# Reads of the memory in the ring of the projections: one PSUM tag changed in an attention and token-mixing kernel

## The chip, the core and the metric

The kernel runs on one core of one Trainium2 chip. The metric is the device time of one execution in microseconds (us). TensorE (PE) multiplies and writes its results into PSUM; VectorE (DVE) and ScalarE (ACT) read them from there; GpSimd (POOL) works on the on-chip memory SBUF; SyncE (SP) issues the DMAs. Each engine runs its own list of instructions in order and waits on semaphores for the others.

## What is computed

A layer norm with modulation, an attention with a compressive memory over four segments, a residual, a second layer norm, and a token-mixing MLP (7 products of a two-level block scheme stand in for its matrix products). Only the attention matters here:

```python
for s in range(N):                       # 4 segments of 512 tokens, 32 heads of 32
    p = softmax(qs @ ks.T * scale + mask)
    a_dot = p @ vs
    pq = phi(qs)                          # phi(t) = t + 1 if t > 0 else exp(t)
    num = pq @ M                          # what the queries read from the memory
    den = pq @ z + 1e-6
    o = g * num / den + (1 - g) * a_dot
    pk = phi(ks)
    M = M + pk.T @ vs                     # the memory's update
    z = z + pk.sum(over tokens)
```

## The kernel before

**Work.** The attention runs over 32 iterations `t`, each of them one group of four heads (`g`) and one segment (`seg`). Iterations 0 to 15 take segments 0 and 1 of the eight groups in turn, iterations 16 to 31 segments 2 and 3. Each iteration has

- a projection (`project`): 96 matmuls for keys and values in two halves (`nps`, L192, 48 each), four transposes of the keys (`kps`, L405) and 24 matmuls for the queries (`qps`, L200). ACT and DVE split each result into a high and a low part (L119, L122). Where the segment is not 0, ACT makes a relu (L416) and an exponential (L417) of the queries and DVE makes `pq` of them (L419);
- the memory (`memory`): for a segment other than 0 two reads `rd` (L450; two halves of two matmuls each) that need `pq` and the memory `MZ`. DVE adds a constant to their denominators (L452), inverts (L453) and multiplies into `am` (L454). Up to segment 2 an update `up` follows (L460, four matmuls), which DVE masks (L462 or L465);
- for each of four heads the maxima (L478 on PE, L480 on DVE; every second head a small transpose `nmps`, L486, and two DMAs of the maxima back into `sk`), the scores (`a`, L515 to L522 on PE; exponentials on ACT; masking, a cast and a subtraction on POOL and ACT, L526 to L530) and the values (`pv`, L544, twenty matmuls; L547 to L551 on DVE), and once an output transpose `ops` (L559).

24 of the 32 iterations have a segment other than 0 and so read the memory: the odd ones up to 15, and all from 16 on.

**PSUM.** There are eight banks, and `bank(tag, bufs, name)` hands them out in rings: `pj` has two, `s1` two (maxima), `s2` two (scores), `pv` one, `ms` one. A tile of a ring of n buffers takes the place of the one that was handed out n calls earlier with the same tag, and its first writer waits until the last reader of that one is done. Before, `pj` carries `nps` half 0, `nps` half 1, `kps`, `qps`, and then `nps` of the next iteration. `ms` carries the two `rd`, `up`, two `nmps` and `ops`.

**Order.** The main loop runs over 128 heads `n`. It calls scores for head `n`, maxima for head `n + 3`, values for head `n - 2` and a piece of the projection for head `n + 8`, so that an iteration is projected two iterations ahead of its scores:

```python
    for n in range(-LEADS, 4 * NI + VL):
        at(scores, n)
        at(maxima, n + LEADS)
        at(values, n - VL)
        m = n + LEADP
        ...
        if m >= 8:
            at(project, m)
```

This gives priorities, not the final order. When the kernel is built, a scheduler goes through a simulated time and gives each engine the first piece that is ready, by the dependencies of tiles and of ring buffers. A dependency that is changed can thus reorder every engine's list.

Of the kernel before, what the change touches and what calls it, by code (L numbers as in the profile page):

```python
# [41 lines left out]
def attention_and_mlp(ctx, tc, x, wq, wkv, wo, beta, w1, b1, w2, b2, c, wm_a, wm_b, out):  # L42
# [19 lines left out]
    a = par.__enter__()  # L62
# [9 lines left out]
    def bank(tag, bufs, name):  # L72
        return psum.tile([P, 512], F32, tag=tag, bufs=bufs, name=name)
# [246 lines left out]
    for i in range(2):  # L320
        ps = bank("s2", 2, f"scps{i}")
# [20 lines left out]
    pj = prj.__enter__()  # L342
# [35 lines left out]
    def project(t, piece):  # L378
# [50 lines left out]
        else:  # L429
# [7 lines left out]
            A.copy(vp[:, :, :, 33:65], r1)  # L437
            V.tensor_tensor(vp[:, :, :, 65:97], r1, vp[:, :, :, 33:65], op=ALU.subtract)
            memory(t)

    def memory(t):
        pr, g, seg = its[t]
        d = st[t]
        d["am"] = am = b.tile([P, 4, 128], F32, tag="am", bufs=3, name=f"am{t}")
        if seg:
            for half in range(2):
                ps = bank("ms", 1, f"rd{t}_{half}")[:, 0:264].rearrange("p (a n) -> p a n", a=2)
                for aa in range(2):
                    i = 2 * half + aa
                    T.matmul(ps[:, aa], d["pq"][:, 128 * i:128 * i + 128], MZ[:, g], start=True, stop=True)  # L450
                rd = b.tile([P, 2, 4], F32, tag="rd", bufs=2, name=f"rdd{t}_{half}")
                V.tensor_scalar_add(rd, ps[:, :, 128:132], 1e-6)  # L452
                V.reciprocal(rd, rd)  # L453
                V.tensor_tensor(am[:, 2 * half:2 * half + 2].rearrange("p a (h e) -> p a h e", h=4),  # L454
                                ps[:, :, 0:128].rearrange("p a (h e) -> p a h e", h=4),
                                rd.unsqueeze(3).to_broadcast([P, 2, 4, 32]), op=ALU.mult)
        if seg < 3:
            ps = bank("ms", 1, f"up{t}")
            for i in range(4):
                T.matmul(ps[:, 0:132], d["pk"][:, i], d["v32"][:, i], start=(i == 0), stop=(i == 3))  # L460
            if seg == 0:
                V.tensor_tensor(MZ[:, g], ps[:, 0:132], bdg[:, g], op=ALU.mult)  # L462
            else:
                tm = b.tile([P, 132], F32, tag="tm", bufs=1, name=f"tm{t}")
                V.tensor_tensor(tm, ps[:, 0:132], bdg[:, g], op=ALU.mult)  # L465
                G.tensor_tensor(MZ[:, g], MZ[:, g], tm, op=ALU.add)
# [132 lines left out]
    def seg_load(seg):  # L599
        seg_x[seg] = [load_x(s2p, tt) for tt in range(4 * seg, 4 * seg + 4)]  # L600
        return norm_all(seg_x[seg])
# [9 lines left out]
    with tc.issue_after(last_wm.ins):  # L611
        _, exp, _, normed_v = seg_load(1)
# [58 lines left out]
    for g in range(2, NG):  # L671
        n = 8 * g - 13
# [5 lines left out]
    for j in range(32):  # L678
        n = ML0 + 2 * j + (8 if j >= 8 else 0)
        later(n, lambda j=j: mod_fetch(j), n + (2 if j < 8 else 1), lambda r, j=j: mod_late(j, r), "V")  # L680
    plan(WO0 - 3, lambda: spread(gaw, 0))
    for i in range(8):
        n = WO0 + WOS * i
        later(n, lambda i=i: wo_fetch(i), n + 1, lambda r, i=i: wo_split(i, r), "G")

    for n in range(-LEADS, 4 * NI + VL):
# [4 lines left out]
        if 0 <= m + 4 < 4 * NI:  # L691
            t = (m + 4) // 4
# [79 lines left out]
    def product(tt):  # L772

        r = wr_.tile([P, NK, P], F32, tag="otr", bufs=1, name=f"otr{tt}")
        SY.dma_start(r, oT[:, :, P * tt:P * tt + P].rearrange("g p n -> p g n"))
        os_ = ws_.tile([P, 2, D], F32R, tag="ots", bufs=2, name=f"ots{tt}")
        for j in range(2):
            split(os_[:, :, 512 * j:512 * j + 512], r[:, 4 * j:4 * j + 4].rearrange("p a b -> p (a b)"), A, V)
        x1 = w.tile([P, D], F32, tag="x1", bufs=2, name=f"x1_{tt}")
        load = SY.dma_start(x1, x[P * tt:P * tt + P])  # L780
        if tt == 1:
            with tc.issue_after(load.ins):
                for c in range(5, NK):
                    SY.dma_start(wop[c, 1].bitcast(F32), wos[c, 1])

        def half(nh):
            ps = bank("pj", 2, f"po{tt}_{nh}")
            n = 0
            for ct in range(NK):
                for i, j in ((0, 0), (0, 1), (1, 0)):  # L790
                    T.matmul(ps, os_[:, i, P * ct:P * ct + P], wop[ct, nh][:, j], start=(n == 0), stop=(n == 3 * NK - 1))  # L791
                    n += 1
            c0, c1 = 512 * nh, 512 * nh + 512
            V.scalar_tensor_tensor(x1[:, c0:c1], ps, 1.0, x1[:, c0:c1], op0=ALU.mult, op1=ALU.add,
                                   accum_out=x1s[:, 2 * tt + nh:2 * tt + nh + 1])
            if nh:
                kept[tt] = SY.dma_start(x1d[tt], x1)

        return half
# [49 lines left out]
    for products, tt in (((0, 1), 0), ((2,), 1), ((3, 4, 8), 8), ((9,), 9), ((10,), 2), ((11,), 10), ((12,), 3),  # L849
# [5 lines left out]
        for i in products:  # L855
            if i > 1:
                f = product(i)
# [283 lines left out]
```

## Time and profile before

| | us |
|---|---|
| runs: median of three (lowest, highest) | 2231.71 (2225.53, 2231.82) |
| the profiled execution's own time | 2226.6 |
| its span | 2224.9 |
| PE busy in the span | 2190.3 (98%) |
| DVE busy | 1666.7 (75%) |
| ACT busy | 1135.7 (51%) |
| POOL busy | 725.8 (33%) |

The attention fills the span up to about 956 us, the output projection follows up to about 1153 us, and the MLP takes the rest. Spans are those of one execution, taken by the hardware profiler. Matmuls are pipelined and their ends are modelled, so that two matmuls in a row overlap in the records. What one costs on PE is the distance to the start of the next.

### The profile page before, as it was taken

How to read it: one execution, taken by the hardware profiler on the slowest of the kernel's cores; microseconds unless marked ns; L12 is line 12 of the kernel's file. 1: busy time of each engine (PE TensorE's matmuls, PEld its weight loads, DVE VectorE, ACT ScalarE, POOL GpSimd, SP SyncE). 2: the span in 40 equal slices, each digit the busy share in tenths (PEclk: the TensorE clock that was granted, in tenths of full speed). 3: DMA queues.
4: the chain of work that ended last, by engine and by line, in shares of the span. 5: the costliest groups of instructions: out<-in, count | busy, mean ns of one | idle time of the engine just before them, and what ended most of it. 6: DMA issues, size and time to landing. Idle time of an engine off the chain costs nothing.

```text
span 2224.9 us, 38052 instructions
## 1 busy us (share of the span) xinstructions
PE 2190.3 (98%) x13786; PEld 1881.0 (85%) x13786; DVE 1666.7 (75%) x3762; ACT 1135.7 (51%) x2050; POOL 725.8 (33%) x831
## 2 busy tenths in 40 slices
PE   8999999999999999999999999999999999999999
PEld 5988898888999999888888888888888888888887
DVE  7676777756777777664858766888888886969687
ACT  5486776756666666654636533533334242424232
POOL 2175766646767776663002200033330000000000
PEclk9999999999999999999999999999999999999999
DMA  7666666686556666664754687655556542414134
GB/s 287 192 187 191 175 181 193 189 279 216 170 180 205 188 183 211 193 219 143 231 194 186 226 304 275 243 223 220 204 202 219 206 148 64 145 57 147 57 123 151
DMA packets 175183, 423.03 MB, mean 190 GB/s; under 512 B 17524, under 2 KB 71828, under 8 KB 166036
## 3 DMA queue, kind: packets, MB, share of 16 engines
q1 hardware_dynamic: 174996, 420.61, 57.5%
q8 instruction: 109, 1.79, 0.3%
q14 instruction: 78, 0.64, 0.1%
HBM read 244.62 MB, written 125.06 MB: 166 GB/s over the span
## 4 chain that ended last, share of the span: by engine, by line
PE 87%; DVE 5%; DMA 3%; ACT 2%; POOL 1%; issue 1%; SPq 0%; DVEq 0%; ACTq 0%
PE mx L921 48%; PE nps L192 11%; PE po L791 8%; PE qps L200 7%; PE pv L544 3%; PE a L515 1%; PE sz L478 1%; PE sx L478 1%; DMA sk<-nt 1%; PE up L460 1%; PE a L518 1%; POOL p L530 1%; PE a L522 1%; PE sy L478 1%; PE rd L450 1%
## 5 line engine op out<-in xcount | busy, mean ns | idle before, releaser
L921 PE MATMUL mx<-bU,sp 128*128 128x512 f32 x2352 | 534.3, 389 | 0.9 <-DVE ac L928 0.9
L921 PEld LDWEIGHTS mx<-bU,sp 128*128 128x128 f32 x2352 | 441.3, 188 | 93.4 <-issue 1.3
L119 ACT CAST sp<-wr 128x384 fp32r<-128x384 f32 (+2 forms) x408 | 218.1, 547 | 431.8 <-PE mx L921 349.1
L192 PE MATMUL nps<-wv,h 128*128 128x256 f32 x3072 | 431.2, 283 | 1.6 <-DVE h L122 0.7
L921 PE MATMUL mx<-bA,sp 128*128 128x512 f32 x1764 | 430.5, 389 | 0.0
L530 POOL TENSOR_TENSOR p<-p,ph 128x640 f16<-128x640 f32 x256 | 380.2, 1485 | 138.5 <-ACT ph L528 134.5
L192 PEld LDWEIGHTS nps<-wv,h 128*128 128x128 f32 x3072 | 400.3, 189 | 9.4 <-DVE h L122 2.0
L921 PEld LDWEIGHTS mx<-bA,sp 128*128 128x128 f32 x1764 | 331.2, 188 | 68.7
L122 DVE TENSOR_TENSOR sp<-wr,sp 128x384 fp32r<-128x384 f32 (+2 forms) x408 | 259.8, 648 | 24.7 <-ACT sp L119 24.4
L928 DVE TENSOR_TENSOR ac<-mx,ac 128x512 f32<-128x512 f32 x280 | 189.9, 687 | 85.2 <-PE mx L921 84.1
L200 PE MATMUL qps<-h,wq 128*128 128x512 f32 x768 | 197.9, 400 | 0.0
L528 ACT CAST ph<-p 128x1280 f16<-128x1280 f32 x128 | 161.4, 1261 | 59.7 <-POOL p L526 59.6
L791 PE MATMUL po<-wo,ots 128*128 128x512 f32 x768 | 180.9, 391 | 0.0
L791 PEld LDWEIGHTS po<-wo,ots 128*128 128x128 f32 x768 | 142.7, 188 | 28.7
L200 PEld LDWEIGHTS qps<-h,wq 128*128 128x128 f32 x768 | 141.6, 190 | 27.7
L921 PE MATMUL mx<-bB,sp 128*128 128x512 f32 x588 | 164.0, 389 | 0.0
L526 POOL TENSOR_SCALAR_AFFINE_SELECT p<-p 128x256 f32<-128x256 f32 x256 | 134.1, 529 | 81.8 <-ACT p L523 53.9
L921 PEld LDWEIGHTS mx<-bB,sp 128*128 128x128 f32 x588 | 110.4, 188 | 22.9
L480 DVE CUSTOM_DVE_ANT_0 sz<-sz,mask 128x512 f32<-128x512 f32 x128 | 89.1, 696 | 52.0 <-PE sz L478 49.5
L480 DVE CUSTOM_DVE_ANT_0 sx<-sx,mask 128x128 f32<-128x128 f32 (+1 forms) x256 | 93.7, 366 | 44.1 <-PE sx L478 37.9
L928 DVE TENSOR_TENSOR cc<-mx,cc 128x512 f32<-128x512 f32 x140 | 94.9, 684 | 37.6 <-PE mx L921 37.4
L516 ACT ACTIVATE p<-a,shift 128x512 f32<-128x512 f32 x128 | 88.4, 691 | 41.2 <-PE a L515 40.4
(209 smaller groups left out, 3244.7 us busy)
## 6 DMA issues: line engine op xcount, KB each, us to landing
sk<-sg SPq DMA_DIRECT2D x384, 128.0 KB
wr<-in_w_dram SPq DMA_DIRECT2D x28, 1024.0 KB
wr<-in_w_dram SPq DMA_DIRECT2D x32, 768.0 KB
bstu<-ucd SPq DMA_DIRECT2D x28, 768.0 KB
wsp<-wv SPq DMA_DIRECT2D x32, 512.0 KB
rawm<-in_wm_b_dram SPq DMA_DIRECT2D x32, 512.0 KB
wv<-wsp SPq DMA_DIRECT2D x32, 512.0 KB
pcd<-cc SPq DMA_DIRECT2D x14, 1024.0 KB
```

Of the source, the lines that this page charges most:

```text
L119: last_hi[0] = A.copy(hi, src)
L122: return lo_eng.tensor_tensor(lo, src, hi.bitcast(F32), op=ALU.subtract)
L192: T.matmul(ps[:, aa], h[:, j, 128 * tt:128 * tt + 128], wt[:, i, o:o + 256], start=(n == 0), stop=(n >= 6 * NK - 2), skip_group_check=True)
L200: T.matmul(ps, wt[:, i, o:o + 128], h[:, j], start=(k + n == 0), stop=(3 * k + n == 3 * NK - 1))
L480: marks[4 * t + h - LEADS, "V"] = V.tensor_tensor_reduce(o, o, mask[:, 384 - 128 * i:], 1.0, -3.0e38, op0=ALU.add, op1=ALU.max, accum_out= ...
L516: A.activation(p32[:, 0:512], b0, AF.Exp, scale=SCALE, bias=shift)
L526: G.affine_select(w, w, pattern=[[0, 2], [1, 128]], compare_op=ALU.is_ge, fill=0.0, base=0, channel_multiplier=-1)
L528: marks[n, "A"] = A.copy(hi, p32)
L530: marks[n, "G"] = G.tensor_tensor(lo[:, c], p32[:, c], hi[:, c], op=ALU.subtract)
L791: T.matmul(ps, os_[:, i, P * ct:P * ct + P], wop[ct, nh][:, j], start=(n == 0), stop=(n == 3 * NK - 1))
L921: T.matmul(ps, ops[q][:, i, P * k:P * k + P], b[:, j], start=(m == 0 and first), stop=(m == 3 * nk - 1), skip_group_check=True)
L928: V.tensor_tensor(d, ps, d, op=ALU.add)
```

## The change

The two reads of an iteration take their PSUM bank from the ring `pj` of two buffers in place of the ring `ms` of one:

```diff
         if seg:
             for half in range(2):
-                ps = bank("ms", 1, f"rd{t}_{half}")[:, 0:264].rearrange("p (a n) -> p a n", a=2)
+                ps = bank("pj", 2, f"rd{t}_{half}")[:, 0:264].rearrange("p (a n) -> p a n", a=2)
                 for aa in range(2):
                     i = 2 * half + aa
                     T.matmul(ps[:, aa], d["pq"][:, 128 * i:128 * i + 128], MZ[:, g], start=True, stop=True)
```

In an iteration that reads, `pj` now hands out six tiles: `nps` 0, `nps` 1, `kps`, `qps`, `rd` 0, `rd` 1. `nps` half 0 of the next iteration takes the bank of `rd` 0, and half 1 that of `rd` 1. `ms` is left with `up`, `nmps` and `ops`. The instructions are the same; the scheduler puts them in another order on every engine, from iteration 1 to the last heads of the attention.

The first place is PE's list in iteration 25 (group 4, segment 3), a few instructions behind its last query matmul. `nps_0_11965` and `nps_1_12090` are the key and value projection of iteration 26, `rd_0_11881` and `rd_1_11888` the two reads of iteration 25, `a_...` scores and `s..._` maxima. Before:

```order
L192 MATMUL nps_0_11965<-wv_5_1_1_11523,h_6_7307 128x256 x4
L450 MATMUL rd_0_11881<-MZ,pq_11802 128x132 x2
L521 MATMUL a_23_2_11708<-sk_2_503 128x128
L522 MATMUL a_23_2_11708<-sk_2_503 128x256
L478 MATMUL sy_3_11920<-sk_3_500 128x384
L515 MATMUL a_23_3_11817<-sk_3_504 128x512
L192 MATMUL nps_0_11965<-wv_5_1_1_11523,h_6_7307 128x256 x2
L192 MATMUL nps_0_11965<-wv_5_1_1_11523,h_7_7762 128x256 x6
L192 MATMUL nps_1_12090<-wv_5_0_0_11517,h_0_6929 128x256 x6
```

and in the changed kernel, at the same reads:

```order
L478 MATMUL sy_3_11920<-sk_3_500 128x384
L515 MATMUL a_24_0_11900<-sk_0_497 128x512
L518 MATMUL a_24_0_11903<-sk_0_497 128x384
L521 MATMUL a_24_0_11906<-sk_0_497 128x128
L522 MATMUL a_24_0_11906<-sk_0_497 128x256
L450 MATMUL rd_0_11881<-MZ,pq_11802 128x132 x2
L450 MATMUL rd_1_11888<-MZ,pq_11802 128x132 x2
L515 MATMUL a_24_1_12029<-sk_1_498 128x512
L478 MATMUL sz_3_11923<-sk_3_500 128x512
L518 MATMUL a_24_1_12032<-sk_1_498 128x384
L478 MATMUL sx_0_12045<-sk_0_501 128x128
L478 MATMUL sx_0_12045<-sk_0_501 128x256
```

Before, 40 of the 48 matmuls of `nps_0_11965` stand ahead of the first read. In the changed kernel all 96 stand behind both reads, and between the last query matmul and the first of them stand only pieces of heads (here three `L515`, three `L518`, two pairs of `L521` and `L522`, three pairs of `sx`, two `sy`, two `sz`, one `nmps` and forty `pv` matmuls) and the reads.

The second place is DVE's list in the same iteration. Before, from the subtraction that makes the low part of the queries (`sg_11764<-qps_11772`) on:

```order
L122 TENSOR_TENSOR sg_11764<-qps_11772,sg_11764 128x512
L436 TENSOR_TENSOR r_25_11874<-v_25_11530,vp_11873 128x512
L489 SCALAR_TENSOR_TENSOR nt_24_1_11731<-nmps_1_11728,nt_24_1_11730 8x128
L419 SCALAR_TENSOR_TENSOR pq_11802<-qps_11772,rq_11799 128x512
L480 ISA sz_2_11841,mx_2_11832<-sz_2_11841,mask 128x512
L480 ISA mx_2_11832 128x1
L573 SCALAR_TENSOR_TENSOR rawm_11813,mcol<-rawm_11813,scb 128x1024
```

In the changed kernel thirteen rows stand between that subtraction and `pq`: two pieces of `sx`, a `sy` and a `sz` with a short row of the accumulator behind each, and `L436`, `L547`, `L489`, `L573` and `L549`. From `pq` to the eviction of the first read it then reads:

```order
L419 SCALAR_TENSOR_TENSOR pq_11802<-qps_11772,rq_11799 128x512
L438 TENSOR_TENSOR vp_11873<-r_25_11874,vp_11873 128x16x32
L480 ISA sy_3_11920,mx_2_11832<-sy_3_11920,mask 128x384
L480 ISA mx_2_11832 128x1
L480 ISA sx_3_11915,mx_2_11832<-sx_3_11915,mask 128x256
L480 ISA mx_2_11832 128x1
L551 SCALAR_TENSOR_TENSOR red_1_11866<-red_1_11866,gate,pv_1_11844 128x128
L452 TENSOR_SCALAR rdd_0_11884<-rd_0_11881 128x8
L453 RECIPROCAL rdd_0_11884<-rdd_0_11884 128x8
L454 TENSOR_TENSOR am_11880<-rd_0_11881,rdd_0_11884 128x256
```

Before, `pq` was third behind the subtraction; now it is fourteenth, because the maxima that PE runs in that stretch have moved ahead of it.

## The prediction

> **What bounds the kernel now.** I first read the busy time by stage (columns: stretch in us, its length, then busy time with the number of instructions for PE, weight loads, DVE, ACT and POOL; then the granted TensorE clock, the DMA share and GB/s), here the two halves of the attention:
>
> ```profile
> 60.00:525.00 465.00, 451.35 (x3898) 412.84 (x3899) 332.56 (x968) 318.06 (x587) 274.71 (x315) 0.99 0.66 197
> 525.00:956.00 431.00, 424.87 (x3845) 391.25 (x3844) 307.87 (x938) 275.05 (x476) 294.52 (x354) 1.00 0.64 194
> ```
>
> PE is busy 451.35 of 465.00 us and 424.87 of 431.00 us, so it waits 13.65 + 6.13 = 19.8 us in the whole attention; DVE and ACT have about a quarter of the time free. The attention lasts as long as PE's list. Whatever leaves PE without work lengthens the kernel, and a shorter wait elsewhere gives back 19.8 us at the very most. Next I read PE's timeline at the place that the change touches, iteration 25, behind its last query matmuls (start, length, engine, line, matmul; the distance from a start to the next is the cost):
>
> ```profile
> 782.27 0.71 PE L200 MATMUL qps<-h,wq 128*128 128x512 f32 x2
> 782.82 0.39 PE L478 MATMUL sx<-sk 96*128 96x128 f32 x2
> 783.05 0.34 PE L478 MATMUL sy<-sk 96*128 96x384 f32 x1
> 783.23 1.78 PE L192 MATMUL nps<-wv,h 128*128 128x256 f32 x14
> ...
> 786.19 0.48 PE L515 MATMUL a<-sk 98*128 98x512 f32 x1
> 786.51 0.34 PE L518 MATMUL a<-sk 98*128 98x384 f32 x1
> 786.68 0.39 PE L478 MATMUL sz<-sk 96*128 96x512 f32 x1
> 786.91 0.44 PE L544 MATMUL pv<-vp,ph 128*128 128x97 bf16 x6
> ...
> 787.50 0.48 PE L478 MATMUL sx<-sk 96*128 96x128 f32 x2
> ...
> 789.76 0.61 PE L450 MATMUL rd<-MZ,pq 128*128 128x132 f32 x4
> 790.12 0.31 PE L521 MATMUL a<-sk 98*128 98x128 f32 x1
> ...
> 790.44 0.34 PE L478 MATMUL sy<-sk 96*128 96x384 f32 x1
> ```
>
> The queries end at 782.27 + 0.71 = 782.98, and at 783.23, after one `sx` and one `sy`, the projection of iteration 26 begins. The reads wait for `pq`, which ACT and DVE make out of those queries; PE runs the projection in the meantime, and the first read comes at 789.76. That is the cover that matters: the 6.8 us from the queries' end to the read are filled with PE work, mostly `nps`.
>
> **The change part by part.** Nothing is removed or added: the same matmuls, evictions and DMAs are issued. What changes is two dependencies, and by them the order.
>
> *First: reads and updates no longer share one bank.* `up` waits no longer for the second read's eviction, nor do `nmps` and `ops` queue behind reads in `ms`. The largest such wait in the trace is this (in brackets the idle time before, and who ended it):
>
> ```profile
> 455.29 2.10 PE L460 MATMUL up<-v,pk 128*128 128x132 f32 x8 [3.48 <-DVE am L454]
> ```
>
> 3.48 us once. I count this gain inside the 19.8 us below and not by itself.
>
> *Second: the next projection waits for the reads.* `nps` half 0 takes the bank of `rd` 0, so its first matmul cannot start before DVE's L454 has read that bank. Behind it on PE stand 96 matmuls and everything after them. In the 24 iterations that read, the order therefore puts only pieces of heads between the last `qps` and the first `nps`, and the question is whether they fill the chain queries, `pq`, read, eviction. The last of the 24 has no `nps` behind it, which leaves 23.
>
> The chain, for iteration 25 in the changed order, by the mean duration of each kind of instruction between 600 and 905 us (number, busy time, then mean ns of one; idle time behind the bar):
>
> ```profile
> L480 DVE CUSTOM_DVE_ANT_0 sz<-sz,mask 128x512 f32<-128x512 f32 x44 | 30.7, 697 | 13.9 <-PE sz L478 13.8
> L573 DVE SCALAR_TENSOR_TENSOR rawm<-rawm,scb 128x1024 f32<-128x1024 f32 x20 | 30.0, 1501 | 6.7 <-DMA rawm<-in_wm_b_dram 6.7
> L480 DVE CUSTOM_DVE_ANT_0 sy<-sy,mask 128x384 f32<-128x384 f32 x44 | 25.3, 575 | 0.9 <-PE sy L478 0.7
> L480 DVE DVE_READ_ACCUMULATOR2_ANT mx<- 128x1 f32 x173 | 24.3, 140 | 0.0
> L549 DVE TENSOR_REDUCE red<-pv 128x128 f32<-128x384 f32 x43 | 23.8, 553 | 1.9
> L480 DVE CUSTOM_DVE_ANT_0 sx<-sx,mask 128x256 f32<-128x256 f32 x43 | 18.8, 437 | 0.4
> L551 DVE SCALAR_TENSOR_TENSOR red<-red,gate,pv 128x128 f32<-128x128 f32 x43 | 14.7, 341 | 0.3
> ...
> L480 DVE CUSTOM_DVE_ANT_0 sx<-sx,mask 128x128 f32<-128x128 f32 x43 | 12.7, 295 | 10.2 <-PE sx L478 9.6 <-PE nmps L486 0.4
> L438 DVE TENSOR_TENSOR vp<-r,vp 128x512 bf16<-128x512 f32 x11 | 9.8, 891 | 0.9 <-ACT vp L437 0.9
> L454 DVE TENSOR_TENSOR am<-rd,rdd 128x256 f32<-128x256 f32 x21 | 8.8, 421 | 0.3
> L436 DVE TENSOR_TENSOR r<-v,vp 128x512 f32<-128x512 f32 x11 | 8.8, 798 | 0.0
> L547 DVE RECIPROCAL pv<-pv 128x4 f32<-128x4 f32 x43 | 8.1, 189 | 19.6 <-PE pv L544 19.3
> ...
> L419 DVE SCALAR_TENSOR_TENSOR pq<-qps,rq 128x512 f32<-128x512 f32 x11 | 7.5, 686 | 1.4 <-ACT rq L417 1.4
> L122 DVE TENSOR_TENSOR sg<-qps,sg 128x512 fp32r<-128x512 f32 x11 | 7.5, 685 | 0.0
> L489 DVE SCALAR_TENSOR_TENSOR nt<-nmps,nt 8x128 fp32r<-8x128 f32 x22 | 6.0, 273 | 0.8 <-ACT nt L488 0.7
> ...
> L453 DVE RECIPROCAL rdd<-rdd 128x8 f32<-128x8 f32 x21 | 4.1, 198 | 0.4
> L452 DVE TENSOR_SCALAR rdd<-rd 128x8 f32<-128x8 f32 x21 | 3.4, 163 | 6.6 <-PE rd L450 6.5
> ```
>
> and from the same view of ACT:
>
> ```profile
> L119 ACT CAST sg<-qps 128x512 fp32r<-128x512 f32 x11 | 6.5, 590 | 3.0 <-PE qps L200 2.9
> ```
>
> DVE's subtraction of the queries' low part can only start when ACT has copied their high part (0.59). From it to `pq`, both included, DVE has: subtraction 0.685, `sx` 0.437, `sy` 0.575, `sz` 0.697, `sx` 0.295 with an accumulator row of 0.140 behind each (0.56), `r` 0.798, reciprocal 0.189, `nt` 0.273, `rawm` 1.501, reduce 0.553, `pq` 0.686, in sum 7.25. From there to the end of the first eviction: `vp` 0.891, `sy` 0.575, `sx` 0.437 and their two accumulator rows 0.28, `red` 0.341, `rdd` 0.163, reciprocal 0.198, `am` 0.421, in sum 3.31. Together 0.59 + 7.25 + 3.31 = 11.1 us, with no wait inside counted. DVE runs its list in order, so none of this can be overtaken.
>
> PE's work in the same stretch, by the distances in the timeline above: three `L515` at 0.32, three `L518` at 0.17, two pairs `L521`/`L522` at 0.32, three pairs of `sx` at 0.23, two `sy` at 0.18, two `sz` at 0.23, forty `pv` at 0.037 (16 of them take 0.59), two halves of the reads at 0.36, and one `nmps` at next to nothing: 0.96 + 0.51 + 0.64 + 0.69 + 0.36 + 0.46 + 1.48 + 0.72 = 5.8 us. PE would stand for 11.1 - 5.8 = 5.3 us. The heads' work that was spread between `nps` matmuls is now bunched, and behind the stretch the 96 `nps` run with little to wait for; PE's own sum is unchanged, so a stall here comes back nowhere.
>
> The bound from the other side is a stall of this shape that the trace already has. In iteration 3 the order happens to put heads between the queries and the next projection:
>
> ```profile
> 124.04 1.78 PE L200 MATMUL qps<-h,wq 128*128 128x512 f32 x7
> ...
> 129.55 0.33 PE L521 MATMUL a<-sk 98*128 98x128 f32 x1 [0.65 <-ACT p L516]
> ...
> 131.02 0.51 PE L515 MATMUL a<-sk 98*128 98x512 f32 x1 [0.52 <-ACT p L519]
> 131.36 0.60 PE L559 MATMUL ops<-ident,am 128*128 128x128 f32 x4
> ...
> 134.09 4.35 PE L192 MATMUL nps<-wv,h 128*128 128x256 f32 x26
> ```
>
> From 124.04 + 1.78 = 125.82 to 134.09 are 8.27 us; what stands between (two `L515`, three `L518`, two pairs `L521`/`L522`, eleven maxima matmuls, 30 `pv`, four transposes at 0.60 together) costs 5.2 us by the prices above. PE stood for 3.1 us, waiting for ACT's exponentials, without any read to wait for. So a stretch costs between 3.1 and 5.3 us. I take 4.5: nearer the upper end because DVE's list is a sum that cannot shrink, not at it because its means were taken while DVE and POOL were both loaded. In 23 stretches that is 104 us.
>
> Some of the 19.8 us that PE waits now lie in these places or vanish with the first part; I take half, -10 us.
>
> *Third: the clock.* Both long stalls of the present trace are followed by a half clock:
>
> ```profile
> 133.00:136.40 3.40, 3.40 (x23) 3.19 (x23) 2.76 (x3) 3.40 (x8) 3.13 (x3) 0.50 1.00 260
> 454.00:464.00 10.00, 8.71 (x45) 7.83 (x46) 7.53 (x26) 4.31 (x9) 4.33 (x9) 0.50 0.99 371
> ```
>
> After the stall of iteration 3 the granted clock is 0.50 for 3.4 us, after the 3.48 us wait it is 0.50 for 10 us. Work at half clock takes double, so a drop costs at least 1.7 us. I assume one such drop behind every second stretch, 23 / 2 x 1.7 = +20 us; the bounds are none and one each (39 us).
>
> The Trainium skill ("TensorE: Matmul & The Clock Gate", Part 1: The HAM clock gate) says that TensorE falls to half its clock after an idle window of about 3.4 us and needs as long a busy one to come back. The trace agrees with the length of the window, 3.40 us at 0.50; but between 129 and 133 us PE was not idle throughout when it happened. By that rule alone stalls broken up by heads would trip nothing, and the sum would be 20 us lower.
>
> **The sum.** 104 - 10 + 20 = +114 us on the profiled execution's 2226.6 us gives 2340.6 us. The median of the runs lies 5.1 us above that execution, so the predicted median is 2346 us, 5.1% more.
>
> **The rivals.**
>
> *The chain is short and the ring of one was the brake (faster).* If `rd` 0 is evicted within the 5.8 us of PE work, `nps` never waits, and the `up` and `nmps` waits are gone. For it: PE's wait of 3.48 us and its half clock of 10 us (5 us lost) both hang on `ms`. Against it: 11.1 us of DVE list. It would give 2231.7 - 8.5 = 2223 us, and with all 19.8 us gained 2212. It decides where the order leaves DVE under about 5 us of list between the subtraction and L454. Chance 0.04. The Trainium skill ("Perfetto Trace Analysis", Optimizing Tensor Performance, Matmuls) asks for just this: independent groups of matmuls should rotate through different PSUM banks, so that the eviction of one overlaps the next. The two reads now do so; that the projection comes to queue behind them, the rule does not say.
>
> *No difference.* The stalls and the waits that go cancel: stretches of about 1 us, 23 us, against 19.8 us gained, 2232 to 2235 us. The 3.1 us of iteration 3 speak against it. Chance 0.04.
>
> *The stall is only that of iteration 3.* 23 x 3.1 = 71, less all 19.8, no clock drops: +51, 2283 us. For it: DVE's means are from a loaded time. Chance 0.18.
>
> *The clock falls behind every stretch and the longer lists decide.* 23 x 5.3 = 122 and 39 of clock, nothing gained: +161, 2393 us; it could go past that, since other iterations have more rows on DVE between subtraction and eviction than iteration 25. Chance 0.12.
>
> The forecast keeps 0.62. The range for 8 in 10 goes from 2275, below the third rival, to 2412, above the last. A measurement of this kernel can tell some 0.3% (6.7 us) from no change. Slower by more than that: 0.62 + 0.18 + 0.12 = 0.92; the same 0.04; faster 0.04.
>
> **What would show it right or wrong.** In the changed profile PE's busy share between 60 us and the attention's end falls from 97 and 99% to about 87%, with the idle time in front of `rd` (released by DVE `pq`), of `nps` (released by DVE `am`) and of the heads' matmuls between the two; the maxima on DVE show no such idle time. The distance from the last `qps` to the first `nps` is 9 to 13 us in iterations that read, and under 3 us in the even ones up to 14. The period of iterations 16 to 30 grows from some 28 to 33 us. The granted clock shows windows of 0.50 in the attention. From the output projection on, nothing changes: the MLP still takes the same 1072 us. I am wrong if the first `nps` of an iteration follows its queries within 7 us, if PE's waits name POOL or DMAs and not DVE, or if the added time lies behind the attention.

## The result and the profile after

| | before | after |
|---|---|---|
| runs: median (lowest, highest), us | 2231.71 (2225.53, 2232.27) | 2352.68 (2347.82, 2358.93) |
| span of the profiled execution, us | 2224.9 | 2346.1 |
| PE busy, us | 2190.3 | 2256.2 |
| DVE busy, us | 1666.7 | 1654.2 |
| mean granted TensorE clock | 0.997 | 0.969 |

The runs are five executions of each kernel. The ratio is 1.0548 (95% interval 1.0524 to 1.0573): the changed kernel is 5.5% slower, 121 us. The forecast of 2346 us lies 7 us below the median and inside the range.

The busy time by stage, for the changed kernel (same columns as before the change: stretch, length, then busy time of PE, weight loads, DVE, ACT and POOL, then the granted clock, DMA share and GB/s):

```profile
60.00:525.00 465.00, 435.64 (x3609) 392.36 (x3609) 303.19 (x895) 302.87 (x553) 251.68 (x292) 0.93 0.62 182
525.00:956.00 431.00, 397.07 (x3270) 353.73 (x3270) 260.23 (x811) 231.08 (x405) 251.74 (x303) 0.93 0.57 170
60.00:1080.00 1020.00, 944.66 (x7777) 845.47 (x7778) 633.21 (x1928) 601.38 (x1075) 570.79 (x674) 0.93 0.59 174
1276.00:2346.00 1070.00, 1065.62 (x4699) 881.23 (x4697) 860.31 (x1442) 409.41 (x757) 99.43 (x64) 1.00 0.50 178
```

The last query matmul of the attention now ends at 1070.8 us, where it ended at 955.6, and the MLP starts at 1274.5 us, where it started at 1153.3. In the third row PE is idle for 1020.00 - 944.66 = 75.3 us, where it was 19.8, and its clock is 0.93, where it was 0.99 to 1.00. The MLP in the last row is untouched. The clock's record has 146.8 us at half speed in the attention, where it had 13.7 (3.4 + 10.2). PE's busy time grew by 2256.2 - 2190.3 = 65.9 us with the same matmuls, half of the 133.1 us of half clock that were added. I therefore count half a microsecond lost for each one at half clock, and the account closes: 75.3 + 146.8 / 2 = 148.7 us lost now, 19.8 + 13.7 / 2 = 26.6 before, a difference of 122.1 against 121.2 us of span.

PE's waits in the changed kernel (who waits for whom; us in total, times, longest):

```profile
PE a L515 <- DMA sk<-nt: 19.5, 15, 2.7
PE sy L478 <- DVE mx L480: 13.2, 21, 1.4
PE sz L478 <- DVE mx L480: 12.2, 14, 2.7
PE sx L478 <- DMA sk<-sg: 9.3, 7, 2.7
...
PE a L521 <- ACT p L516: 5.4, 9, 2.2
PE sx L478 <- DVE mx L480: 2.8, 4, 0.9
...
PE rd L450 <- DVE pq L419: 2.0, 2, 1.8
...
PE nps L192 <- DVE am L454: 0.9, 2, 0.7
```

The two waits that the change makes, `rd` for `pq` and `nps` for `am`, hold only 2.9 us. The rest hangs on the heads' pieces that the order has put ahead of the projection: maxima whose bank DVE has not yet read (28.2 us), and scores and maxima whose operands come by DMA (28.8 us). That looks as if the reads had nothing to do with it. PE's timeline of iteration 25 shows how it fits together (start, length, engine, line, matmul; in brackets the idle time before and who ended it):

```profile
864.17 2.70 PE L200 MATMUL qps<-h,wq 128*128 128x512 f32 x11
866.70 0.39 PE L515 MATMUL a<-sk 98*128 98x512 f32 x1
...
869.24 0.50 PE L478 MATMUL sx<-sk 96*128 96x128 f32 x2
871.00 0.44 PE L478 MATMUL sy<-sk 96*128 96x384 f32 x1 [1.26 <-DVE mx L480]
872.25 0.76 PE L515 MATMUL a<-sk 98*128 98x512 f32 x1 [0.81 <-DMA sk<-nt]
872.82 0.52 PE L518 MATMUL a<-sk 98*128 98x384 f32 x1
873.80 0.47 PE L521 MATMUL a<-sk 98*128 98x128 f32 x1 [0.46 <-ACT p L516]
874.07 0.52 PE L522 MATMUL a<-sk 98*128 98x256 f32 x1
874.39 1.96 PE L450 MATMUL rd<-MZ,pq 128*128 128x132 f32 x8
876.00 0.78 PE L515 MATMUL a<-sk 98*128 98x512 f32 x1
...
878.41 0.46 PE L544 MATMUL pv<-vp,p 128*128 128x65 bf16 x10
878.71 0.48 PE L192 MATMUL nps<-wv,h 128*128 128x256 f32 x2
```

The queries end at 866.87 and the first `nps` comes at 878.71, 11.8 us later; before the change it came 0.25 us later. Each idle piece stands in front of a head's matmul, and the work after it runs at half clock: the reads take 1.6 us to the next start, where 0.72 was reckoned, and one `L515` shows 0.76 where 0.39 is normal. DVE in the same place (same columns):

```profile
867.58 0.69 DVE L122 TENSOR_TENSOR sg<-qps,sg 128x512 fp32r<-128x512 f32 x1
...
870.81 1.21 DVE L573 SCALAR_TENSOR_TENSOR rawm<-rawm,scb 128x1024 f32<-128x1024 f32 x1
...
872.64 0.67 DVE L419 SCALAR_TENSOR_TENSOR pq<-qps,rq 128x512 f32<-128x512 f32 x1
...
875.51 0.17 DVE L452 TENSOR_SCALAR rdd<-rd 128x8 f32<-128x8 f32 x1 [0.43 <-PE rd L450]
875.71 0.20 DVE L453 RECIPROCAL rdd<-rdd 128x8 f32<-128x8 f32 x1
875.95 0.42 DVE L454 TENSOR_TENSOR am<-rd,rdd 128x256 f32<-128x256 f32 x1
```

DVE works without a gap from 867.37 to 875.08. `pq` is ready 6.4 us and the first `am` 9.5 us after the queries' end. I read this as DVE's list setting the pace, for the maxima and for the reads alike, while the projection that used to stand here cannot start.

Over the 23 stretches between the last `qps` and the next first `nps`, summed from the trace's records (after, and in brackets before): mean length 13.31 us (1.16), DVE busy in 90% of it, PE idle 68.7 us in all (2.3), at half clock 138.8 us (1.1). The stretches of the iterations that do not read stay short (0.25 to 2.6 us, the first one 4.8).

The same records show the new dependency, although the list of waits hardly names it. In all 23 stretches the first `nps` starts after the first `am` is done: on average `pq` is ready 7.2 us after the queries' end, `am` 12.5 us, and `nps` starts at 13.3. Before, it started ahead of `am` in all 23, and ahead of `pq` in 22. Only 0.8 us of the mean stretch lie behind the eviction.

### The profile page after: what moved, and what is told of

The parts are those of the page before. It is cut to its first block, busy times and chain, and to the rows that moved or that the text cites. A ratio compares the mean times of both kernels' runs of the same rounds, so it can differ in the third digit from the quotient of the medians.

```text
span 2346.1 us, 37990 instructions
## 1 busy us (share of the span) xinstructions
PE 2256.2 (96%) x13786; PEld 1921.7 (82%) x13786; DVE 1654.2 (71%) x3762; ACT 1134.8 (48%) x2050; POOL 721.1 (31%) x831
## 4 chain that ended last, share of the span: by engine, by line
PE 88%; DVE 6%; DMA 2%; ACT 1%; issue 1%; SPq 0%; DVEq 0%; ACTq 0%
PE mx L921 45%; PE nps L192 14%; PE po L791 7%; PE qps L200 7%; PE pv L544 3%; PE a L515 1%; PE rd L450 1%; PE sz L478 1%; DMA sk<-nt 1%; PE sx L478 1%; PE up L460 1%; PE a L518 1%; PE a L522 1%; PE srow L294 1%; DVE sx L480 1%
## 5 line engine op out<-in xcount | busy, mean ns | idle before, releaser
L192 PE MATMUL nps<-wv,h 128*128 128x256 f32 x3072 | 396.7, 282 | 2.4 <-DVE am L454 0.9
L192 PEld LDWEIGHTS nps<-wv,h 128*128 128x128 f32 x3072 | 375.9, 189 | 6.8 <-DVE h L122 2.0
L480 DVE CUSTOM_DVE_ANT_0 sx<-sx,mask 128x128 f32<-128x128 f32 (+1 forms) x256 | 93.5, 365 | 127.3 <-PE sx L478 126.3
L523 ACT ACTIVATE p<-a,shift 128x384 f32<-128x384 f32 x128 | 74.7, 583 | 82.7 <-PE a L522 80.8
```

What stands on the lines that cost most here:

```text
L192: T.matmul(ps[:, aa], h[:, j, 128 * tt:128 * tt + 128], wt[:, i, o:o + 256], start=(n == 0), stop=(n >= 6 * NK - 2), skip_group_check=True)
L480: marks[4 * t + h - LEADS, "V"] = V.tensor_tensor_reduce(o, o, mask[:, 384 - 128 * i:], 1.0, -3.0e38, op0=ALU.add, op1=ALU.max, accum_out= ...
L523: A.activation(p32[:, 896:1280], b2_[:, 0:384], AF.Exp, scale=SCALE, bias=shift)
```

## The experiments

In the expectations, A is the theory of the prediction: the next projection queues behind a read's eviction, the heads' work fills only part of that time, and the rest is lost on PE. The other letters are rivals, each as its expectation tells it. The results of all runs in one table; the "stretch" is the mean distance from the last `qps` to the next first `nps` in the 23 places, and the half clock is the total of the drops that reach into the trace from 60 to 1200 us:

| run | median us | ratio to before (95%) | stretch us | half clock us |
|---|---|---|---|---|
| the change | 2352.68 | 1.0548 (1.0524 to 1.0573) | 13.31 | 146.8 |
| e1, change in the second pass only | 2313.77 | 1.0385 (1.0365 to 1.0404) | 8.89 | 109.2 |
| e2, reads after the next projection | 2252.55 | 1.0106 (1.0085 to 1.0127) | 1.18 | 27.3 |
| e3, one of two reads moved | 2327.35 | 1.0445 (1.0426 to 1.0464) | 9.33 | 122.9 |
| e4, three extra passes, changed | 2477.03 | 1.1117 (1.1097 to 1.1137) | 20.63 | 310.6 |
| e5, three extra passes, before | 2268.72 | 1.0169 (1.0146 to 1.0191) | 1.29 | 41.0 |
| e6, clock kept up | 2370.52 | 1.0629 (1.0613 to 1.0645) | 13.19 | 34.1 |
| e7, reads in the maxima's ring | 2242.28 | 1.0056 (1.0038 to 1.0074) | 1.16 | 10.2 |
| e8, `up` moved in place of the reads | 2298.00 | 1.0308 (1.0292 to 1.0324) | 8.15 | 102.4 |
| e9, late reads in the old ring | 2275.16 | 1.0197 (1.0176 to 1.0217) | 0.62 | 37.5 |
| e10, one extra pass, changed | 2379.88 | 1.0661 (1.0642 to 1.0679) | 15.21 | 167.3 |
| e11, three banks, reads elsewhere | 2331.25 | 1.0444 (1.0429 to 1.0460) | 1.23 | 109.2 |
| e12, three banks, reads in `pj` | 2346.54 | 1.0507 (1.0489 to 1.0525) | 9.94 | 126.3 |

**e1: the change in iterations 16 to 31 only.**

```diff
-                ps = bank("pj", 2, f"rd{t}_{half}")
+                ps = bank(*(("pj", 2) if pr else ("ms", 1)), f"rd{t}_{half}")
```

> Only the 16 reads of iterations 16 to 31 use the projections' ring; the 8 of the first pass stay where they were. Theory A (each stretch between the queries and the next projection waits for DVE's list from the queries' subtraction to the read's eviction): the cost is one per stretch, and the 15 of the second pass cost what its periods grew by in the changed kernel, 503.3 - 430.3 = 73 us: about 2305 us (2292 to 2318). Theory C (the new order of the whole attention is worse, whatever waits for what): no such sum; anything between 2232 and 2353 us.

Measured: 2313.77 us, within A's interval. 3.85% of 2232 us is 86 us in 15 stretches, 5.7 us each; the other 5.48 - 3.85 = 1.63%, 36 us, belongs to the 8 stretches of the first pass, 4.5 us each. The cost goes roughly with the number of stretches, not with their length alone: in the changed kernel those of the first pass are longer (15.0 us on average, 12.4 in the second) and lose more on PE (7.8 us by idle time and half of the half clock, against 5.0). Why they still cost less was not followed up.

**e2: the reads moved behind the next projection.** The reads of an iteration are called after the second half of the next projection, still in `pj`. Since the update of the memory must not overtake them, POOL first copies the memory into `bd` where an update follows.

```diff
+            if piece == 1 and t:
+                reads(t - 1)
...
+        if 0 < seg < 3:
+            G.tensor_copy(bd, MZ[:, g])
...
-                    T.matmul(ps[:, aa], d["pq"][:, 128 * i:128 * i + 128], MZ[:, g], start=True, stop=True)
+                    T.matmul(ps[:, aa], d["pq"][:, 128 * i:128 * i + 128], M, start=True, stop=True)
```

> The reads of an iteration keep the projections' ring, but are called after both halves of the next iteration's keys and values (a copy of the memory, made on POOL ahead of the update, keeps what they read), so that the next projection no longer stands behind them in the ring; the next keys' transposes do. Theory A: the stretch is filled with projection matmuls again and the loss is gone: 2222 to 2242 us, the half clocks gone too. Theory B (sharing the two banks is itself the cost) and theory C: most of the loss stays, over 2290 us.

Measured: 2252.55 us, 10 us above the upper end of A and far from the rivals. PE's timeline at one of its reads:

```profile
796.78 6.66 PE L200 MATMUL qps<-h,wq 128*128 128x512 f32 x20
803.27 0.40 PE L532 MATMUL a<-sk 98*128 98x512 f32 x1
...
805.00 1.99 PE L192 MATMUL nps<-wv,h 128*128 128x256 f32 x16
...
817.78 2.96 PE L192 MATMUL nps<-wv,h 128*128 128x256 f32 x23
820.57 0.61 PE L463 MATMUL rd<-MZ,pq 128*128 128x132 f32 x4
```

The same two reads stand in the same ring, but a whole projection stands between the queries and them. What comes next in the ring, the transposes of the keys and the queries, hardly waits; its largest wait for a read's eviction is that of the queries (us in total, times, longest):

```profile
PE qps L200 <- DVE am L467: 1.8, 3, 0.8
```

About four fifths of the loss are gone (5.48% to 1.06%). So it is not the ring or the bank as such that costs, but which tile comes next in the ring and how early.

**e9: the control for e2**, with the late reads in `ms` as before the change.

```diff
-                ps = bank("pj", 2, f"rd{t}_{half}")
+                ps = bank("ms", 1, f"rd{t}_{half}")
```

> Control for the second experiment: the same late reads and the same copy of the memory by POOL, but the reads' bank comes from the ring ms as before the change. A (the ring of the projections costs nothing once the reads come late; the 21 us that were left there belong to the late reads and the copy): 2240 to 2262, within 0.5% of 2252.6. B (some of the 21 us are still the ring): 2226 to 2238.

Measured: 2275.16 us, above both. That the 21 us left in e2 belong to the late reads and the copy is right in sign, but the old ring is 0.9% worse here than `pj`, and the intervals do not touch. Once the reads come late, moving them out of `ms` gains about 20 us. The Trainium skill ("Perfetto Trace Analysis", Optimizing Tensor Performance, Matmuls) wants independent groups in different banks; the pair e2 and e9 agrees with it, and the change as it was made does not.

**e3: only the second of the two reads in `pj`.**

```diff
-                ps = bank("pj", 2, f"rd{t}_{half}")
+                ps = bank(*(("pj", 2) if half else ("ms", 1)), f"rd{t}_{half}")
```

> Only the second half's read uses the projections' ring. The first half of the next projection then takes the bank of the queries, and waits for pq, not for a read's eviction. Theory A: DVE's list from the subtraction to pq takes 0.6 + 7.3 us against some 4.1 us of PE work in the new order's stretch, 3.8 us per stretch against 5.3: by the measured loss of 121 us for 5.3, about 87 us, 2305 to 2325 us. Theory C: with half of the reads moved, half of the loss, 2290 us, or all of it, 2350 us.

Measured: 2327.35 us, 2 us above A's interval. One read in the ring costs 4.45 of the 5.48%. The trace shows that it does so in another way than two reads: half 0 of the next projection takes the bank of the queries, and in all 23 stretches its first `nps` starts after `pq` (7.0 us after the queries' end) and ahead of the first `am` (11.9). PE loses 4.1 us a stretch by idle time and half of the half clock, where A reckoned 3.8 and where the change loses 6.0. So most of the cost comes as soon as one more tile in the ring shifts the projection onto the bank of the queries.

**e7: both reads in the ring of the maxima, `s1`.**

```diff
-                ps = bank("pj", 2, f"rd{t}_{half}")
+                ps = bank("s1", 2, f"rd{t}_{half}")
```

> The reads leave the memory's bank for the two banks of the maxima. Theory A: nothing of the projection waits for a read, some 48 of its matmuls stand ahead of the first read again, and the time is near that of before: 2225 to 2255 us; if the single shared bank was a brake, below 2225. Theory C: any move of the reads disturbs the order and costs over 1.5%, over 2265 us.

Measured: 2242.28 us, as A expects. Putting the reads among the maxima costs 0.56%, a tenth of the change, and its mean stretch is as short as before. A relief of `ms` brings no gain that shows here; the run cannot tell it from what the reads cost in the ring of the maxima.

**e8: the reads stay in `ms`, and the memory's update goes to `pj`.**

```diff
-            ps = bank("ms", 1, f"up{t}")
+            ps = bank("pj", 2, f"up{t}")
```

> The reads stay where they were; the memory's update uses the projections' ring in its place. Theory A: now the next projection waits for the update's masking on DVE in the 24 iterations that update, behind ACT's two passes over the keys and pk on DVE; the order again puts no projection matmul ahead of the reads in iterations 11 to 15 and in segment 2: a loss of the same kind, 2280 to 2345 us. If it is the reads' own chain through the queries that counts, under 2260 us.

Measured: 2298.00 us, within A's interval, but not for the reason that it gives. With one more tile in the ring, half 0 of the next projection takes the bank of the queries, as in e3, and only half 1 that of `up`. In the 16 iterations that both read and update, the first `nps` starts after `pq` each time, the mean stretch is 11.0 us, and PE loses 16 x 4.8 = 77 us there by idle time and half of the half clock, against 69 us measured for the whole run. In the seven that read without an update the stretch is 1.6 us. Of the eight that update without a read, seven have 2.6 to 3.1 us, and only the first of the kernel is long (14.4). So it is again the wait for `pq` that is seen, not the update's own masking.

**e4 and e5: a longer list on DVE.** Three passes are added behind `pq` that leave it as it is (the maximum of `pq` with itself), in the changed kernel and in the one before.

```diff
+                for _ in range(3):
+                    V.tensor_tensor(d["pq"], d["pq"], d["pq"], op=ALU.max)
```

> The changed kernel with three more DVE passes over pq (the maximum with itself, each about 0.69 us) ahead of the reads. Theory A: 2.1 us more in each of 23 stretches, 35 to 50 us: 2385 to 2405 us. Theory D (the stretch is as long as PE's own work at half clock, not DVE's list): at most 15 us more.

> The kernel before with the same three more DVE passes over pq. Theory A: they lie under the projection's matmuls and cost next to nothing: 2229 to 2242 us. If the order of before too stands close to the end of its cover, more than 2245 us.

Both missed A's intervals on the same side; in e5 the other branch, more than 2245 us, is what came. The changed kernel lost 5.69% more (127 us), and the one before 1.69% (38 us). The direction is A's, since the same work costs three times as much behind the change; the sizes are not. Duration of the passes in the changed kernel (ns: lowest, median, highest):

```profile
L421 DVE TENSOR_TENSOR pq<-pq x72: 670/897/1947, 84.8 to 1212.8; 128x512 f32<-128x512 f32 x72
```

and in the kernel before with the same passes:

```profile
L421 DVE TENSOR_TENSOR pq<-pq x72: 667/690/1960, 84.0 to 1002.5; 128x512 f32<-128x512 f32 x72
```

and DVE's timeline in one iteration of the changed kernel with them:

```profile
977.89 0.69 DVE L419 SCALAR_TENSOR_TENSOR pq<-qps,rq 128x512 f32<-128x512 f32 x1
...
980.62 0.88 DVE L421 TENSOR_TENSOR pq<-pq 128x512 f32<-128x512 f32 x1
...
984.19 0.67 DVE L421 TENSOR_TENSOR pq<-pq 128x512 f32<-128x512 f32 x1
...
985.68 1.78 DVE L421 TENSOR_TENSOR pq<-pq 128x512 f32<-128x512 f32 x1
```

The three passes take 3.3 us but the last ends 8.9 us after `pq` is done (987.46 against 978.58), because each depends on the one before and the order puts rows of the heads between. The stretch grew by 7.3 us on average, not by 2 to 3. The added dependent steps are dearer than their durations. In the kernel before, the 6.8 us of cover are not enough for all of it, which I had assumed: there `rd` waits for the last of the passes (us in total, times, longest):

```profile
PE rd L452 <- DVE pq L421: 5.7, 4, 2.6
```

**e10: the same with one pass.**

> The changed kernel with one extra pass of DVE over pq (it leaves pq as it is) where the fourth experiment had three. A with bare prices (a pass costs its own duration, 0.67 to 0.9 us, in 23 stretches): 2353 + 15 to 21 = 2368 to 2374. C (each dependent step of DVE also queues behind other rows that the order puts between, as the +124 us for three passes suggests, 41 us a pass): 2385 to 2402.

Measured: 2379.88 us; by the ratios 1.13% more than the change, 25 us or 1.1 us a stretch, between the two expectations. One pass has a median of 0.82 us in that run and lengthens the stretch by 1.9 us; three lengthen it by 7.3, so the price of a step is not constant either.

**e6: the clock kept up.** Behind the maxima of heads 2 and 3 of each stretch, three matmuls of the mask with itself go into the `ms` bank, whose result nobody reads.

```diff
+            if h >= 2 and t + 1 < NI and its[t + 1][2]:
+                spin = bank("ms", 1, f"spin{t}_{h}_{tiles[0]}")
+                with tc.issue_after(mm.ins):
+                    for _ in range(3):
+                        T.matmul(spin, mask[:, 0:128], mask, start=True, stop=True)
```

> The changed kernel with three idle matmuls (zeros, into the bank of the maxima's transposes, read by nobody) behind each of the six groups of maxima matmuls that fall into a stretch, so that PE is busy where it would wait for DVE. Theory A: the granted clock in the stretches rises, but their length is DVE's list: within 12 us of the changed kernel, 2340 to 2365 us. Theory D (half clock is the cost): 25 to 60 us less, 2290 to 2328 us.

Measured: 2370.52 us; D's interval is missed by 42 us, and A's by 5.5 us. The attention and one of the fillers with what follows it:

```profile
60.00:1090.00 1030.00, 985.31 (x8183) 843.94 (x8183) 627.22 (x1913) 597.42 (x1070) 569.58 (x672) 0.99 0.58 171
```

```profile
890.37 0.81 PE L483 MATMUL spin<-mask 128*128 128x512 bf16 x3
891.02 0.26 PE L549 MATMUL pv<-vp,p 128*128 128x65 bf16 x3
```

The clock is 0.99 and the half clock is down from 146.8 to 34.1 us, a loss of some 56 us less by the account above. The time did not fall by it: the stretch stayed at 13.19 us, and the first `am` came 12.1 us after the queries' end, where it had come at 12.5. But the filler is no free probe. It is 144 groups of three at 0.65 us (890.37 to 891.02), 94 us of PE work; 309 of its 432 matmuls ran in the stretches, 2.9 us in each, about as much as the half clock had taken there (3.0 us). It cost 18.6 us of span. So the run shows that idle work does not buy the time back, and that the chain to the eviction hardly changes with the clock. That the half clock is only what a PE without enough work looks like, and not a price on top, is argued from this and not shown.

**e11 and e12: three banks for the projections.** `ms` is given up, its tiles go to `s1`, and `pj` gets three banks. In e11 the reads go to `s1`, in e12 to `pj`; against the changed kernel every `pj` and every `ms` of e12 is renamed in this way:

```diff
-                ps = two_tiles(bank("pj", 2, f"nps{t}_{half}"))
+                ps = two_tiles(bank("pj", 3, f"nps{t}_{half}"))
...
-            ps = bank("ms", 1, f"up{t}")
+            ps = bank("s1", 2, f"up{t}")
```

> Base for the next run: ms is given up, its tiles and the reads go to the ring s1, and pj has three banks. No read stands in the ring of the projections. A: 2225 to 2275 (the small tiles queue among the maxima).

> As the run before, but the reads go to pj, which has three banks: half 0 of the next projection now takes the bank of the queries and waits for pq, and only half 1, 48 matmuls later, waits for a read's eviction. A (what costs is the chain that the first nps waits for; it ends at pq, 7.8 of the 11.1 us): 45 to 90 us above the run before. B (a third bank takes the wait away): within 20 us of it. C (any place in that ring costs the same): 105 us or more above it.

The base e11 is already 4.4% slower and far above its expectation, although its mean stretch is short (1.23 us; only iterations 3 and 9 are long, 14.6 and 7.3): giving up `ms` for a third bank in `pj` costs by itself. e12 lies 0.63%, 14 us, above it, which misses A and is nominally B, but on a base with 109 us of half clock and a moved order this tells nothing of the wait. Only the stretch can be read: 9.94 us where the first `nps` takes the bank of the queries and starts after `pq` in all 23 places, 13.31 where it takes that of a read. On the time the pair is inconclusive.

## Why the prediction was right

**No instructions are added, so what counts is the order: right.** The account of idle time and half clock closes without any growth of PE's work, the MLP is unchanged, and all 121 us lie ahead of the MLP, 115 of them ahead of the attention's last query matmul.

**The stretch: right in kind, and longer than reckoned.** The mechanism is as forecast: `nps` starts after the eviction in all 23 places. I forecast 9 to 13 us for the reading iterations; 14 of the 23 are in that interval and nine above it (10.4 to 18.9, mean 13.31, the longest in iteration 9). The chain to the first `am` has a mean of 12.5 us where I summed 11.1 for iteration 25, and with the 6.0 us lost a stretch taken off, PE has 13.31 - 6.0 = 7.3 us of work in it at full clock where I counted 5.8. In iteration 25 the chain itself was shorter than its sum: `pq` at 6.4 us (7.8 reckoned), `am` at 9.5 (11.1). The first `nps` still came at 11.8, because the order had put scores, maxima and `pv` between the reads and it, and PE ran them at half clock (876.00 to 878.41). Iterations 16 to 30 have a mean period of 33.5 us (28.7 before); I had said 33 from 28.

**The terms of the sum: the total is right, the split is not.**

| term | predicted us | measured us |
|---|---|---|
| PE idle in the 23 stretches | +104 | 68.7 - 2.3 = +66.4 |
| half clock | +20 (0 to 39) | in the stretches (138.8 - 1.1) / 2 = +68.9 |
| stalls elsewhere that go | -10 | -13.2 |
| sum | +114 | +122.1 |

The last measured figure is what idle time and half clock outside the stretches lost before (23.8) and lose now (10.6). The step that was mis-sized is the third, the clock: "I assume one such drop behind every second stretch". There were 24 drops of 3.4 to 13.7 us, nearly every stretch had one, and they lie in the stretch, not behind it: of the 146.8 us only 1.1 fall into the projections between two stretches and 6.8 behind the last one. The idle term was mis-sized the other way, as I read it for the same reason: heads' matmuls at half clock fill time in which PE would otherwise stand. I take idle time and half clock as one quantity here, which e6 suggests and does not prove: 135.3 / 23 = 5.9 us each, where 4.5 and 0.87 were predicted. The 5.3 us that I had as the upper bound of a stall, without any term for the clock or for stalls that go, would have given 23 x 5.3 = 122. That it meets the measured 121 so closely is luck, and so in part is the forecast's total: chain and work were both reckoned too short, and the terms for idle time and clock missed by 38 and 49 us in opposite directions. The lower bound was read wrongly too: in the stretch of iteration 3 before the change PE is idle for 1.6 us and 1.1 us are at half clock, 2.1 us lost, where the prices had given 3.1.

**Who ends the waits: partly wrong.** I expected idle time in front of `rd`, `nps` and the heads' matmuls, named DVE, and wrote that waits which name POOL or DMAs and not DVE would prove me wrong. The list above names both: DVE 31.1 us (maxima 28.2, `rd` 2.0, `nps` 0.9), DMAs 28.8 and ACT 5.4. The DMAs carry the maxima and the split heads into `sk`, so a head's own chain is exposed too when nothing of the projection is there to cover it. In e2, where the projection is back, PE's waits for those DMAs hold 13.7 us; e4 and e10 show that a longer list of DVE ahead of the reads lengthens the stretch. How much of a stretch the heads' chains would still take if the reads' chain were shorter was not separated; e3, where `nps` is let go at `pq`, still loses 4.1 us a stretch. PE's busy share did not fall to 87% but to 944.66 / 1020 = 92.6%, since PE at half clock counts as busy.

**The rivals.** That the ring of one was the brake is refuted for the change as it was made, and reads that leave it for the ring of the maxima (e7) bring 0.56% more time, not less. "No difference" and "only 3.1 us" fell with the measured 5.3 us of span a stretch (121.2 / 23). The case "clock behind every stretch" had the count of drops about right (23, where there were 24), but put them behind the stretches, while they lie in them.

**What stays open.** Why late reads cost 1 to 2% (e2, e9), though no stretch is long and the half clock is only 27 to 38 us, and why the extra passes of e4 have a median of 0.90 us against 0.69 in e5, the runs do not tell.

## What to carry to other kernels

When a tile moves into another ring, ask which tile takes its bank next and how late its last reader is: a small result that is evicted late stops the large group behind it, and one tile more in the ring already moves that group onto another bank (e3, e8). The waits then show up under the names of whatever the scheduler put in between. Take the stall from the length of the chain on the slower engine less the work that covers it, count idle time and half clock as one loss, and price each dependent step of that chain above its own duration. If such a tile must share a ring, put the large group ahead of it, as e2 does; here that still cost 1.06% against leaving the reads where they were.

## What the runs showed of the hardware

The clock's steps in the changed kernel all lie on one grid: every drop is a multiple of 3.413 us from every other. Stretches along that grid (columns as above):

```profile
137.51:140.92 3.41, 2.58 (x19) 1.41 (x17) 3.34 (x14) 3.41 (x6) 0.99 (x3) 1.00 1.01 394
140.92:144.33 3.41, 1.93 (x7) 1.01 (x7) 2.90 (x7) 2.51 (x5) 3.41 (x5) 0.50 0.46 127
523.21:526.62 3.41, 1.87 (x17) 1.67 (x15) 0.00 (x0) 1.83 (x4) 3.33 (x3) 1.00 0.94 308
526.62:530.03 3.41, 2.85 (x33) 2.62 (x34) 1.88 (x8) 2.22 (x4) 0.65 (x2) 1.00 0.76 262
867.96:871.37 3.41, 2.13 (x21) 1.34 (x19) 3.41 (x11) 3.41 (x8) 2.65 (x5) 1.00 0.38 78
871.37:874.79 3.42, 2.15 (x7) 1.49 (x7) 3.42 (x12) 1.87 (x4) 1.91 (x3) 0.50 0.40 87
874.79:878.20 3.41, 3.41 (x19) 3.12 (x18) 2.82 (x12) 1.68 (x2) 2.46 (x4) 0.50 0.92 196
878.20:881.61 3.41, 3.41 (x42) 3.39 (x40) 2.02 (x8) 1.30 (x3) 3.33 (x3) 1.00 0.49 105
```

A window in which PE is busy for 2.13 of 3.41 us (62%) is followed by half clock, and the clock comes back after a window of 3.41. The Trainium skill ("TensorE: Matmul & The Clock Gate", Part 1: The HAM clock gate) tells of a free-running window of about 3.4 us, and the grid agrees. It speaks of an idle window; in this trace the windows ahead of a drop were busy for 15 to 76%, half of them for over 50%, and from 60 us on the windows that kept the full clock were busy for 55% and more (the third row, 1.87 of 3.41). Between 55 and 76% the busy time alone does not decide. By the word idle, stalls broken up by heads would have tripped nothing, as the forecast noted; here they did so in nearly every stretch.
